# A gated mix of linear attention and a token-shift MLP on one core: the first four x tiles loaded as column slices and four query tiles accumulated side by side

## The chip, the cores and the metric

The kernel runs on one core of a Trainium2 chip. The metric is the device time of one execution in microseconds (us). Before the change the median of three runs is 259.72 us (259.62 to 259.99).

## The reference, cut to what matters

```python
x = A_x                                                 # 2048 x 640, bfloat16
g = sigmoid((x * gate_w).sum(-1, keepdims=True))
a = linear_attention(x, wqkv, wo)                       # phi(q), phi(k), 32 heads of 20
b = mixer_mlp(x, w1, w2, w3, w4)                        # layernorm, w1, shifts, w2, layernorm, w3, w4
return g * a + (1 - g) * b
# in linear_attention: qkv = x @ wqkv; phi(t) = where(t > 0, t + 1, exp(t)) + 1e-6
```

The change touches only the start of the attention branch: the loading of x and of the query and key parts of wqkv, the turning of x (TensorE needs x with its 640 features on the partitions), and the first query products x @ wq.

## The kernel before, in words

The 2048 tokens are 16 tiles of 128; the 640 features are 5 column blocks k of 128 (KD = 5). One query tile is five matmuls, one for each k, 128 x 512, added up in one PSUM bank: the stationary operand is the block xT[:, k, tile], the moving one wq[:, k, 0:512]. One key tile is five matmuls of 512 columns and five of 130 in a pair of banks. After its last matmul a query tile goes through `phi` (lines 788 to 796): an Exp on ScalarE, a TENSOR_SCALAR and a SCALAR_TENSOR_TENSOR on VectorE; only then is its bank free. The last 128 query columns are done for four tiles together (`q_turned`).

xT comes in two ways. For tiles 0 to 2 `t_x` (lines 777 to 786) transposes the five blocks on TensorE against an identity (`tr_group`, L615, five transposes in one bank) and VectorE copies them out of PSUM (`copy`, L669). For tiles 3 to 15 `x_turn` (line 689) has SP issue a DMA transpose as soon as the tile's load has landed. In the same bank as tile 2's transposes one small matmul turns the gate weights (line 782), and VectorE casts the result into wkg (line 786).

Every instruction is recorded by `_Sched`, which adds the semaphore waits that its reads, writes and PSUM banks need. Each engine then works off its own list strictly in the order recorded. `_Items.run` (line 336) decides that order from estimated costs: the stream "A" (lines 944 to 960) is warm-up matmuls without a use for the result (`warmup`, WARM = 3456 columns), t_x(0), 128 warm-up columns, then `q_three` (query tiles 0 to 2), `k_two` (key tiles 0 and 1), key tile 2, and from tile 3 on a query tile and a key tile in turn, with the turned query columns after every fourth key tile. Inside `q_three` and `k_two` the order is written out by hand as pairs (tile, k) and worked off by `stream` (line 906); there (t, None) means "turn tile t now".

Loads are issued in the order of lines 694 to 718, from the SP queue and the ACT queue. x tiles 0 to 3 are four loads of 160 KB each, in pieces of 1280 bytes; the five blocks wq[:, k, 0:512] are 128 KB each, in pieces of 1024 bytes; the five blocks of wk are 160 KB each.

`IT.add("QN", ...)` at line 1359 only makes the later scaling of the queries wait for the item that holds the first query tiles.

Of the kernel before, what the change touches and what calls it, by code (L numbers as in the profile page):

```python
# [11 lines left out]
D = 640  # L12
# [5 lines left out]
KD = D // 128  # L18
# [398 lines left out]
def _build(nc, A_x, A_wqkv, A_wo, B_w1, B_w2, B_w3, B_w4, gate_w, out, dbg=None, stop=None):  # L417
# [42 lines left out]
    ps = nc.alloc_psum_tensor("ps", [128, 8, 512], F32)  # L460
    sch.register(ps, "ps", 8 * PS_BANK, 0)

    def psb(b, n0, n1):
        return ps[:, b, :].bitcast(BF16)[:, n0:n1]
# [53 lines left out]
    def bank():  # L518
        best = None
        for k_ in range(nbanks[0]):  # L520
            b = (bank_rr[0] + k_) % nbanks[0]
            if b in bank_pend or b in bank_hold:
                continue
            lk = sch.locks.get(b)
            tfree = 0.0 if lk is None else sch.ev_time.get((lk[1].sem, lk[1].val), 1e18)
            if best is None or tfree < best[0]:
                best = (tfree, b)
        bank_rr[0] = best[1] + 1
        bank_pend.add(best[1])
        return best[1]  # L530
# [67 lines left out]
    def mm_group(out_ap, pairs, reads_extra=()):  # L598
        n = len(pairs)

        def fn(e, out_ap=out_ap, pairs=pairs, n=n):
            ins = None
            for i, (l, r) in enumerate(pairs):
                ins = e.matmul(out_ap, l, r, start=(i == 0), stop=(i == n - 1))  # L604
            return ins
        reads = [a for p in pairs for a in p] + list(reads_extra)
        return pe(fn, reads, [out_ap], cost=n * (max(nfree(pairs[0][1]), 24) * 0.4167 + 2.5))

    def tr_group(b, srcs):
        outs = [psb(b, 128 * i, 128 * (i + 1)) for i in range(len(srcs))]  # L610

        def fn(e, outs=outs, srcs=srcs):
            ins = None
            for o, s_ in zip(outs, srcs):
                ins = e.transpose(o, s_, ident[:])  # L615
            return ins
        return pe(fn, list(srcs) + [ident[:]], [psb(b, 0, 128 * len(srcs))], cost=len(srcs) * 56.0)
# [47 lines left out]
    def copy(engf, out_ap, in_ap):  # L665
        cost = None
        if engf is dve and in_ap.dtype == BF16 and out_ap.dtype == BF16:
            cost = 65.0 + nfree(out_ap) / 1.92
        return engf(lambda e: e.tensor_copy(out_ap, in_ap), [in_ap], [out_ap], cost=cost)  # L669
# [5 lines left out]
    x2 = A_x[0]  # L675

    def dma_in(out_ap, in_ap, key, **kw):
        return sch.dma("sp", out_ap, in_ap, key, **kw)

    def load_x(t):  # L680
        dma_in(x_tok[:, t, :], x2[128 * t:128 * (t + 1), :], "x%d" % t)

    def load_wq(k, queue):
        sch.dma(queue, wq[:, k, 0:512], A_wqkv[128 * k:128 * (k + 1), 0:512], "wq%d" % k)

    def load_wk(k, queue):
        sch.dma(queue, wkg[:, k, 0:D], A_wqkv[128 * k:128 * (k + 1), D:2 * D], "wk%d" % k)

    def x_turn(t):
        sch.dma("sp", xT[:, :, 128 * t:128 * (t + 1)], x_tok[:, t, :], "trx%d" % (t % 4), transpose=True)  # L690

    gwr = xn[:, 1, 0:128]
    dve(lambda e: e.memset(gwr, 0.0), [], [gwr])
    load_x(0)
    load_wq(0, "act")
    load_x(1)
    load_wq(1, "act")
    load_wq(2, "sp")
    load_wq(3, "act")
    load_x(2)  # L700
    load_wq(4, "act")
    load_wk(0, "sp")
    load_wk(1, "act")
    load_x(3)
    load_wk(3, "act")
    sch.dma("act", wq[:, :, 512:D], A_wqkv[:, 512:D].rearrange("(k p) f -> p k f", p=128), "wqt")
    load_wk(2, "sp")
    load_wk(4, "sp")
    load_x(4)
    x_turn(3)  # L710
    load_x(5)
    sch.dma("pool", xn[0:KD, 1, 0:128], gate_w.rearrange("(k p) -> k p", p=128), "gw")
    x_turn(4)
# [60 lines left out]
    WARM = 3456  # L774
    WARM2 = 128

    def t_x(t):
        for k0, k1 in ((0, 1), (1, KD)) if t < 2 else ((0, KD),):
            b = bank()
            tr_group(b, [x_tok[:, t, 128 * k:128 * (k + 1)] for k in range(k0, k1)])  # L780
            if t == 2:
                mm_group(ps[:, b, 448:448 + KD], [(gwr, ident[:, 0:KD])])
            for j0, j1 in {(1, 1): ((1, 3), (3, KD)), (2, 0): ((0, 2), (2, KD))}.get((t, k0), ((k0, k1),)):
                copy(dve, xT[:, j0:j1, 128 * t:128 * (t + 1)], psb(b, 128 * (j0 - k0), 128 * (j1 - k0)).rearrange("p (k c) -> p k c", k=j1 - j0))
            if t == 2:
                copy(dve, wkg[:, :, D + 1:D + 2], ps[:, b, 448:448 + KD].rearrange("p (k o) -> p k o", o=1))

    def phi(b, dst, after_exp=None, n=D):
        se = slot("E", 3)
# [86 lines left out]
    def warmup(cols, cyc):  # L876
        b = bank()
        one = nc.const_aps.tensor(1.0, [128, 512], BF16)
        steps = [512] * (cols // 512) + [128] * (cols % 512 // 128)

        def fn(e):
            ins = None
            for n in steps:
                ins = e.matmul(ps[:, b, 0:n], one[:, 0:128], one[:, 0:n], start=True, stop=True)  # L884
            return ins
        pe(fn, [], [ps[:, b, :]], cost=cols * cyc)
# [13 lines left out]
    def q_tile(t):  # L900
        tok = slice(128 * t, 128 * (t + 1))
        b = bank()
        mm_group(ps[:, b, :], [(xT[:, k, tok], wq[:, k, 0:512]) for k in range(KD)])
        phi(b, pq_tok[:, t + 1, 0:512], n=512)

    def stream(order, w, n2, done):
        bs = {}
        for t in sorted({t for t, k in order if k is not None}):
            bs[t] = pair() if n2 else bank()
            bank_hold.update((bs[t], bs[t] + 1) if n2 else (bs[t],))  # L910
        for t, k in order:
            if k is None:
                if t is None:
                    warmup(256, 0.42)
                else:
                    t_x(t)
                continue
            b = bs[t]
            l = xT[:, k, 128 * t:128 * (t + 1)]

            def fn(e, l=l, b=b, k=k):
                ins = e.matmul(ps[:, b, 0:512], l, w[:, k, 0:512], start=(k == 0), stop=(k == KD - 1))  # L922
                return ins if not n2 else e.matmul(ps[:, b + 1, 0:n2], l, w[:, k, 512:512 + n2], start=(k == 0), stop=(k == KD - 1))  # L923
            pe(fn, [w[:, k, 0:512 + n2], l], [ps[:, b, 0:512]] + ([ps[:, b + 1, 0:n2]] if n2 else []), cost=272.0 if n2 else 216.0)
            if k == KD - 1:
                bank_hold.difference_update((b, b + 1) if n2 else (b,))
                done(t, b)

    def q_three():
        order = [(0, 0), (1, None), (0, 1), (1, 0), (1, 1), (0, 2), (1, 2), (0, 3), (1, 3), (2, None), (0, 4), (1, 4),  # L930
                 (2, 0), (2, 1), (2, 2), (2, 3), (2, 4)]
        stream(order, wq, 0, lambda t, b: phi(b, pq_tok[:, t + 1, 0:512], n=512))

    def k_out(t, b):
# [6 lines left out]
    def addA(name, dur, fn, deps=()):  # L941
        IT.add("A", name, dur, fn, deps)
# [1 line left out]
    addA(("warm",), 0.0, lambda: warmup(WARM, 0.834))  # L944
    addA(("tx", 0), 0.28, lambda: t_x(0))
    addA(("warm", 1), 0.0, lambda: warmup(WARM2, 0.42))
    addA(("q", 2), 3.24, q_three)
    addA(("k", 1), 2.72, k_two)
    addA(("k", 2), 1.36, lambda: k_tile(2))
    for i in range(3, NT + 2):  # L950
        if i < NT:
            addA(("q", i), 1.08, lambda t=i: q_tile(t))
            addA(("k", i), 1.36, lambda t=i: k_tile(t))
            if i % 4 == 3:
                addA(("qx", i // 4), 1.08, lambda c=i // 4: q_turned(c))
                IT.add("QB", ("qb", i // 4), 0.0, lambda c=i // 4: q_back(c),
                       deps=[(("qx", i // 4), 2.5), (("t1", NT - 1), 0.0) if i == NT - 1 else (("k", i + 1), 0.0)])
        if i > 3:
            for t in range(3) if i == 4 else (i - 2,):
                addA(("g0", t), 0.27, lambda t=t: gt_tail(t), deps=[(("k", max(t, 1)), 2.0)])  # L960
# [355 lines left out]
    for t in range(NT):  # L1316
        c = t // 4
# [38 lines left out]
                    IT.add("W3", ("w3h", c2), 1.14, lambda c2=c2: w3_half(c2), [(("t2", u), 0.9) for u in range(4 * c2 + 4, 4 * c2 + 8)] + [(("a", 3), 0.0)])  # L1356
                IT.add("W3", ("w4h", 0), 0.76, lambda: w4_half(0), [(("w4load",), 0.0), (("a", 3), 0.0)])
    for t in range(NT):
        deps = [(("zb",), 1.0), (("q", max(t, 2)), 2.0), (("sg", 1), 0.0)]
        deps.append((("qb", t // 4), 3.0))  # L1360
        if t < 5:
            i = 4 * t + 3
            deps.append((("w1", i // KD, i % KD), 0.0))
        else:
            i = 3 * (t - 5)
            if t >= 12:
                deps.append((("w4", t - 12), 0.0))
            if t < 12:
                deps.append((("w3", i // KFF, i % KFF), 0.0))
        IT.add("QN", ("qs", t), 0.0, lambda t=t: qn_sum(t), deps)  # L1370
        IT.add("QN", ("qn", t), 0.0, lambda t=t: qn_scale(t), [(("qs", t), 0.0)])
        IT.add("QT", ("qt", t), 0.0, lambda t=t: qt_tile(t), deps=[(("qn", t), 3.2), (("w2", NT - 1), 0.5), (("t2", 11 if t < 6 else NT - 1), 0.0)] + ([(("mt",), 0.0)] if t == 3 else []))
# [70 lines left out]
```

## Time and profile before

| what | value |
|---|---|
| median of three runs | 259.72 us (259.62 to 259.99) |
| time of the profiled execution | 259.2 us |
| its span, first to last instruction | 257.9 us |
| TensorE (PE) busy | 255.1 us, 99% |
| VectorE (DVE), ScalarE (ACT), GpSimd (POOL) busy | 56%, 42%, 35% |
| moved by DMA | 26.50 MB, mean 103 GB/s over the span |
| DMA share and rate from 2.0 to 9.0 us | 1.00 to 1.12 in the four windows asked for, 302 to 349 GB/s |

The profile shows one execution. Times in it count from the start of the span. "PE" is the matmul, "PEld" the loading of a stationary operand, which overlaps PE; SPq and ACTq are the issuing of DMAs on these two queues. A matmul's duration runs to its modelled end and overlaps the next one's start, so what a matmul costs in a row of matmuls is the distance between two starts.

### The profile page before, as it was taken

How to read it: one execution, taken by the hardware profiler on the slowest of the kernel's cores; microseconds unless marked ns; L12 is line 12 of the kernel's file. 1: busy time of each engine (PE TensorE's matmuls, PEld its weight loads, DVE VectorE, ACT ScalarE, POOL GpSimd, SP SyncE). 2: the span in 40 equal slices, each digit the busy share in tenths (PEclk: the TensorE clock that was granted, in tenths of full speed). 3: DMA queues.
4: the chain of work that ended last, by engine and by line, in shares of the span. 5: the costliest groups of instructions: out<-in, count | busy, mean ns of one | idle time of the engine just before them, and what ended most of it. 6: DMA issues, size and time to landing. Idle time of an engine off the chain costs nothing.

```text
span 257.9 us, 3904 instructions
## 1 busy us (share of the span) xinstructions
PE 255.1 (99%) x1478; PEld 126.7 (49%) x1478; DVE 144.8 (56%) x289; ACT 108.9 (42%) x224; POOL 90.9 (35%) x144
## 2 busy tenths in 40 slices
PE   8999999999999999999999999999999999999996
PEld 4555555544454545555444445444444744444744
DVE  2697888899964995589999300399700033200033
ACT  1587676651366868666854331001540100253100
POOL 5020499976952162677908000123200021300000
PEclk9999999999999999999999999999999999999999
DMA  7856699956637699372628630114130022200012
GB/s 226 226 135 114 188 137 177 262 109 126 127 76 79 125 399 293 84 100 56 121 49 117 123 60 3 31 25 127 36 17 0 3 52 80 102 1 3 0 20 102
DMA packets 57650, 26.50 MB, mean 103 GB/s; under 512 B 48884, under 2 KB 56221, under 8 KB 57632
## 3 DMA queue, kind: packets, MB, share of 16 engines
q1 hardware_dynamic: 54800, 21.87, 40.2%
q0 software_dynamic: 1168, 3.28, 5.8%
q10 hardware_dynamic: 1664, 1.11, 1.4%
q8 instruction: 11, 0.18, 0.3%
q14 instruction: 7, 0.06, 0.1%
HBM read 12.04 MB, written 2.62 MB: 57 GB/s over the span
## 4 chain that ended last, share of the span: by engine, by line
PE 99%; DVE 0%; issue 0%
PE ps L604 53%; PE ps L1213 30%; PE ps L811 8%; PE ps L922 2%; PE ps L884 1%; PE ps L1240 1%; PE ps L1128 1%; PE ps L615 1%; PE ps L1009 0%; PE ps L1038 0%; PE ps L923 0%; DVE x_tok L643 0%
## 5 line engine op out<-in xcount | busy, mean ns | idle before, releaser
L604 PE MATMUL ps<-xnT,w 128*128 128x512 bf16 x360 | 81.3, 379 | 0.0
L643 DVE SCALAR_TENSOR_TENSOR x_tok<-ps,stg,abx 128x512 bf16<-128x512 f32 (+2 forms) x17 | 12.2, 718 | 81.4 <-PE ps L1213 81.3
L660 ACT ACTIVATE h2T<-ps 128x512 bf16<-128x512 f32 x52 | 30.6, 598 | 59.5 <-PE ps L604 59.5
L604 PEld LDWEIGHTS ps<-xnT,w 128*128 128x128 bf16 x360 | 34.5, 98 | 39.8 <-issue 0.5
L1213 PE MATMUL ps<-w,h2T 128*128 128x512 bf16 (+2 forms) x221 | 45.4, 366 | 0.0
L626 POOL TENSOR_SCALAR xn<-x_tok,st 128x640 bf16<-128x640 bf16 x32 | 36.0, 1130 | 25.4 <-DMA xnT<-xn 24.9
L626 POOL TENSOR_SCALAR abx<-x_tok,stg 128x640 f32<-128x640 bf16 x16 | 15.3, 965 | 70.7 <-DVE x_tok L643 70.7
L1213 PEld LDWEIGHTS ps<-w,h2T 128*128 128x128 bf16 x221 | 21.2, 98 | 23.5
L660 ACT ACTIVATE Er<-ps 128x512 bf16<-128x512 f32 (+1 forms) x36 | 23.0, 649 | 14.6 <-PE ps L604 10.3
L659 ACT ACTIVATE junk<-x_tok 128x640 bf16<-128x640 bf16 x32 | 23.6, 738 | 3.9 <-DVE x_tok L641 3.7
L660 ACT ACTIVATE hsT<-ps 128x512 bf16<-128x512 f32 (+1 forms) x32 | 19.0, 594 | 12.5 <-PE ps L604 12.0
L604 PE MATMUL ps<-w,hsT 128*128 128x512 bf16 (+1 forms) x160 | 23.7, 299 | 0.0
L604 PE MATMUL ps<-wkg,xT 128*128 128x130 bf16 (+1 forms) x140 | 21.4, 299 | 0.0
L641 DVE SCALAR_TENSOR_TENSOR x_tok<-ps,x_tok 128x640 bf16<-128x640 f32 x16 | 13.1, 821 | 11.2 <-PE ps L604 10.5
L604 PEld LDWEIGHTS ps<-w,hsT 128*128 128x128 bf16 x160 | 13.3, 98 | 12.3
L1213 PE MATMUL ps<-M_sb,pqnT 128*128 128x512 bf16 (+2 forms) x85 | 18.6, 367 | 0.0
L811 PE MATMUL ps<-pk_tok,x_tok 128*128 128x512 bf16 x80 | 17.8, 379 | 0.0
L604 PEld LDWEIGHTS ps<-wkg,xT 128*128 128x128 bf16 x140 | 11.9, 97 | 11.4
L1157 DVE TENSOR_TENSOR pq_tok<-pq_tok,dnr 128x300 bf16<-128x300 bf16 (+1 forms) x48 | 16.9, 405 | 0.5
L634 DVE TENSOR_TENSOR qprod<-qprod,pk_tok 128x640 f32<-128x640 f32 x13 | 16.3, 1252 | 0.4
L626 DVE TENSOR_SCALAR Er<-Er 128x512 bf16<-128x512 bf16 (+1 forms) x36 | 12.3, 341 | 6.9 <-ACT Er L660 6.2
L604 PE MATMUL ps<-wq,xT 128*128 128x512 bf16 x65 | 16.2, 379 | 0.0
(87 smaller groups left out, 243.8 us busy)
## 6 DMA issues: line engine op xcount, KB each, us to landing
w<-in_B_w_dram SPq DMA_DIRECT2D x1, 2160.0 KB, 8.1
w<-in_B_w_dram SPq DMA_DIRECT2D x1, 2080.0 KB, 15.2
out_dram<-x_tok SPq DMA_DIRECT2D x3, 640.0 KB, 3.2
w<-in_B_w_dram POOLq DMA_DIRECT2D x8, 160.0 KB, 6.4
x_tok<-in_A_x_dram SPq DMA_DIRECT2D x6, 160.0 KB, 3.7
x_tok<-in_A_x_dram SPq DMA_DIRECT2D x1, 960.0 KB, 5.3
wv<-in_A_wqkv_dram POOLq DMA_DIRECT2D x1, 800.0 KB, 5.7
x_tok<-in_A_x_dram SPq DMA_DIRECT2D x1, 640.0 KB, 4.6
```

The lines of the kernel that those rows point to most:

```text
L604: ins = e.matmul(out_ap, l, r, start=(i == 0), stop=(i == n - 1))
L615: ins = e.transpose(o, s_, ident[:])
L626: return engf(lambda e: e.tensor_scalar(out_ap, in_ap, s1, s2, op0, op1), rd, [out_ap], cost=cost)
L634: return engf(lambda e: e.tensor_tensor(out_ap, a, b_, op), [a, b_], [out_ap], cost=cost)
L641: return dve(lambda e: e.scalar_tensor_tensor(out_ap, in0, scalar, in1, op0, op1, accum_out=accum), rd, [out_ap, accum], cost=cost + 70.0)
L643: return dve(lambda e: e.scalar_tensor_tensor(out_ap, in0, scalar, in1, op0, op1), rd, [out_ap], cost=cost)
L659: return act(lambda e: e.activation(out_ap, in_ap, func, bias=bias, scale=scale, accum_out=accum), rd, wr, cost=cost)
L660: return act(lambda e: e.activation(out_ap, in_ap, func, bias=bias, scale=scale), rd, wr, cost=cost)
L811: ins = e.matmul(o, l, r, start=(t0 + q_ == 0), stop=(t0 + q_ == NT - 1))
L922: ins = e.matmul(ps[:, b, 0:512], l, w[:, k, 0:512], start=(k == 0), stop=(k == KD - 1))
L1157: dve(lambda e, o=o, i0=i0, i1=i1: e.tensor_tensor(o, i0, i1, ALU.mult), [i0, dnr[:, 1, sd, :]], [o], cost=cost)
L1213: ins = e.matmul(o, l, r, start=first and i == 0, stop=last and i == len(prs) - 1, skip_group_check=True)
```

## The change

x tiles 0 to 3 are loaded by three DMAs, each with a slice of the columns of all four tiles: block 0 (128 KB in pieces of 256 bytes), blocks 1 and 2 (256 KB in pieces of 512 bytes), blocks 3 and 4 (the same). They stand on SP; wq's blocks 0 to 2 stand beside them on ACT, and all wq loads are on ACT now. wk's blocks 0, 2 and 4 follow on SP. `x_turn(3)` is gone.

`t_x(k)` now turns block k of four tiles: four transposes in one bank, and a copy of 512 columns (for block 0 a copy of 128 and one of 384). The gate weights' matmul and cast are in t_x(3). `q_three` becomes `q_four`, with the four banks of query tiles 0 to 3 open together and (None, k) for "turn block k now"; the single query tile 3 that stood between key tiles 2 and 3 is gone.

```diff
-    load_x(0)
-    load_wq(0, "act")
-    load_x(1)
-    load_wq(1, "act")
-    load_wq(2, "sp")
+    for i, (k0, k1) in enumerate(((0, 1), (1, 3), (3, KD))):
+        dma_in(x_tok[:, 0:4, 128 * k0:128 * k1], x2[0:512, 128 * k0:128 * k1].rearrange("(n p) d -> p n d", p=128), "xs%d" % i)
+        load_wq(i, "act")
     load_wq(3, "act")
-    load_x(2)
+    load_wk(0, "sp")
     load_wq(4, "act")
-    load_wk(0, "sp")
+    load_wk(2, "sp")
     load_wk(1, "act")
-    load_x(3)
+    load_wk(4, "sp")
     load_wk(3, "act")
     sch.dma("act", wq[:, :, 512:D], ...)
-    load_wk(2, "sp")
-    load_wk(4, "sp")
     load_x(4)
-    x_turn(3)
     load_x(5)
...
+    def t_x(k):
+        b = bank()
+        tr_group(b, [x_tok[:, t, 128 * k:128 * (k + 1)] for t in range(4)])
+        if k == 3:
+            mm_group(ps[:, b, 448:448 + KD], [(gwr, ident[:, 0:KD])])
+        for j0, j1 in ((0, 1), (1, 4)) if k == 0 else ((0, 4),):
+            copy(dve, xT[:, k, 128 * j0:128 * j1], psb(b, 128 * j0, 128 * j1))
+        if k == 3:
+            copy(dve, wkg[:, :, D + 1:D + 2], ps[:, b, 448:448 + KD].rearrange("p (k o) -> p k o", o=1))
...
-        order = [(0, 0), (1, None), (0, 1), (1, 0), (1, 1), (0, 2), (1, 2), (0, 3), (1, 3), (2, None), (0, 4), (1, 4),
-                 (2, 0), (2, 1), (2, 2), (2, 3), (2, 4)]
+        order = [(0, 0), (1, 0), (None, 1), (2, 0), (3, 0), (0, 1), (1, 1), (None, 2), (2, 1), (3, 1), (0, 2), (1, 2), (None, 3), (2, 2),
+                 (None, 4), (3, 2)] + [(t, k) for t in range(4) for k in (3, 4)]
...
-    addA(("q", 2), 3.24, q_three)
+    addA(("q", 3), 4.32, q_four)
...
-            addA(("q", i), 1.08, lambda t=i: q_tile(t))
+            if i > 3:
+                addA(("q", i), 1.08, lambda t=i: q_tile(t))
...
-        deps = [(("zb",), 1.0), (("q", max(t, 2)), 2.0), (("sg", 1), 0.0)]
+        deps = [(("zb",), 1.0), (("q", max(t, 3)), 2.0), (("sg", 1), 0.0)]
```

After the key tiles 2 and 3 the instructions of the changed program stand in the same order as before on TensorE, to the end.

More of the change, by code (lines that the diff above doesn't have):

```diff
@@ L775, in _build @@
     WARM2 = 128
[L777 to L786, printed above, removed]
+    def t_x(k):
[7 more added lines that the diff above has]
+            copy(dve, wkg[:, :, D + 1:D + 2], ps[:, b, 448:448 + KD].rearrange("p (k o) -> p k o", o=1))
     def phi(b, dst, after_exp=None, n=D):
@@ L907, in stream @@
         bs = {}
-        for t in sorted({t for t, k in order if k is not None}):
+        for t in sorted({t for t, k in order if t is not None}):
             bs[t] = pair() if n2 else bank()
@@ L911, in stream @@
         for t, k in order:
[L912 to L916, printed above, removed]
+            if t is None:
+                t_x(k)
                 continue
@@ L927, in stream, with q_four @@
                 done(t, b)
-    def q_three():
-        order = [(0, 0), (1, None), (0, 1), (1, 0), (1, 1), (0, 2), (1, 2), (0, 3), (1, 3), (2, None), (0, 4), (1, 4),
-                 (2, 0), (2, 1), (2, 2), (2, 3), (2, 4)]
+    def q_four():
+        order = [(0, 0), (1, 0), (None, 1), (2, 0), (3, 0), (0, 1), (1, 1), (None, 2), (2, 1), (3, 1), (0, 2), (1, 2), (None, 3), (2, 2),
+                 (None, 4), (3, 2)] + [(t, k) for t in range(4) for k in (3, 4)]
         stream(order, wq, 0, lambda t, b: phi(b, pq_tok[:, t + 1, 0:512], n=512))
```

## The prediction, made before the changed kernel ran

> **What bounds the kernel now.** I read the page's busy times and its chain, then the chain in order of time, then the timeline of the first 9 us, then the DMA issues of that stretch.
>
> ```profile
> PE 255.1 (99%) x1478; PEld 126.7 (49%) x1478; DVE 144.8 (56%) x289; ACT 108.9 (42%) x224; POOL 90.9 (35%) x144
> ...
> PE 99%; DVE 0%; issue 0%
> ```
>
> TensorE is the bound from end to end. A busy PE need not be a full one, so I looked at the distances between matmul starts: after 8.96 us, where the first key matmul starts, none shows a wait. What counts is when that first key matmul starts, and how much PE work is left then. The chain in order of time gives the prices:
>
> ```profile
> 3.87 0.53 PE ps L615 x5
> ...
> 5.50 1.67 PE ps L922 x7
> 7.17 0.28 PE ps L615 x5
> ...
> 20.00 2.44 PE ps L604 x15
> ...
> 25.43 3.52 PE ps L604 x20
> ```
>
> Five transposes take 0.53 us early and 0.28 later: 0.107 and 0.056 each. The clock doubles in between. Of 20.00 and 25.43 the difference is one group of five 128x512 matmuls, 1.08 us: 0.216 each; cold it is 0.43 (the warm-up's weight loads stand at 2.07, 2.49, 2.92). Matmul starts keep the cold distance until 5.3 and have the warm one from 5.71.
>
> The second thing to see is what a transpose costs before its result can be used:
>
> ```profile
> 4.09 0.31 PE L615 MATMUL ps<-ident,x_tok 128*128 128x128 bf16 x1
> ...
> 4.38 0.59 PE L922 MATMUL ps<-wq,xT 128*128 128x512 bf16 x1
> ```
>
> ```profile
> 4.01 0.22 DVE L669 COPY xT<-ps 128x128 bf16<-128x128 bf16 x1 [3.03 <-PE ps L615]
> 4.44 0.43 DVE L669 COPY xT<-ps 128x512 bf16<-128x512 bf16 x1 [0.20 <-PE ps L615]
> ...
> 7.52 0.55 DVE L669 COPY xT<-ps 128x256 bf16<-128x256 bf16 x2 [1.49 <-PE ps L604]
> 8.00 0.17 DVE L669 CAST wkg<-ps 128x5 bf16<-128x5 f32 x1
> ```
>
> ```profile
> 7.29 0.17 PE L604 MATMUL ps<-ident,xn 128*128 128x5 bf16 x1
> ...
> 7.87 0.76 PEld L922 LDWEIGHTS ps<-wq,xT 128*128 128x128 bf16 x5 [0.45 <-DVE xT L669]
> ...
> 8.96 0.38 PE L922 MATMUL ps<-wkg,xT 128*128 128x512 bf16 x1
> ```
>
> A copy starts 0.35 us after the last transpose's start when cold (4.09 to 4.44), 0.23 when warm (7.29 to 7.52). 512 columns take 0.43. The weight load follows 0.05 to 0.08 after the copy's end (the first copy of 7.52 lasts 0.29, to 7.81; the load starts at 7.87). So warm it is 0.23 + 0.43 + 0.07 = **0.73 us from the last of four transposes to the first matmul with them**, 0.90 from the first. Before the change almost all of this lies under other matmuls: the one wait left is 0.12 us (the matmul before 7.87 started at 7.53 and occupies 0.216).
>
> **The change, part by part.** Times from the span's start; t1 is the start of the second slice's transposes, r that of block 3's.
>
> *Start.* The warm-up stays and holds PE until 3.68, where tile 0's transposes now start; x tile 0 landed 2.8 us after its issue at 0.79. If slice 0 is no later, four cold transposes start at 3.68 to 4.00, the first copy runs 4.35 to 4.57, and matmul (0,0) starts 0.15 later (as 4.24 to 4.38), at 4.72. Two cold matmuls of 0.43 end at 5.58. The 128 warm-up columns fill 0.11 of the gap; some 0.4 us of PE idles.
>
> *Slice 1.* Its transposes need blocks 1 and 2 of all four tiles. All loads share a DMA side that is full (share 1.00 to 1.12 from 2 to 9 us):
>
> ```profile
> x_tok<-in_A_x_dram SPq DMA_DIRECT2D x1, 160.0 KB, 2.8
> ```
>
> ```profile
> x_tok<-in_A_x_dram SPq DMA_DIRECT2D x1, 160.0 KB, 4.3
> wq<-in_A_wqkv_dram SPq DMA_DIRECT2D x1, 128.0 KB, 4.0
> ```
>
> These are tile 0, and the third and fourth SP loads: wq's block 2 issued at 1.71, tile 2 at 2.18, so landing at 5.7 and 6.5. SP had then brought 448 and 608 KB; tile 1, at 4.3, made 320. Slice 1 completes 384 KB on SP. Bounds: 4.3, and 6.5 if short pieces slow it. I take 5.75, the wq row that stands nearest, so t1 = 5.80. Slice 2 completes 640 KB: between tile 2 (6.5) and tile 3 (3.13 + 5.6 = 8.7); I take 7.4. It is needed at r.
>
> *The side-by-side order, warm.* Block 1: four transposes (0.22), (2,0) and (3,0) (0.43): PE is through at t1 + 0.65, but (0,1) can start at t1 + 0.90. **Bubble 0.25.** (0,1), (1,1) to t1 + 1.33. Block 2 the same: bubble 0.25, (0,2) at t1 + 2.23, (1,2) done at t1 + 2.66 = r = 8.46. Block 3: transposes to r + 0.22, gate matmul 0.03, (2,2), block 4's transposes, (3,2) to r + 0.90: there (0,3) is just ready. VectorE, however, copies block 3 from r + 0.40 to 0.83, casts the gate to 1.00, and only then copies block 4, to 1.43; (0,4) starts at r + 1.50, where (0,3) ended at 1.12. **Bubble 0.38.** Then seven matmuls from (0,4) on, 1.51: the first key matmul starts at r + 3.01 = **11.47**. Check: from 5.80, 16 transposes 0.89, 18 matmuls 3.88, gate 0.03, bubbles 0.88: 5.68.
>
> *What is saved.* The lone query tile 3: five matmuls, 1.08 us. The old program, with that tile ahead, would have its keys at 8.96 + 1.08 = 10.04. **Net: 11.47 - 10.04 = +1.43 us**, all of it on the path, since no later wait of PE's can absorb it.
>
> *Moved, priced at nothing.* The DMA transpose of tile 3 (1.30 us of SP, from 8.75) goes; behind it tiles 5 and 4 come no later, and tile 4's turned x, needed at about 18 us, was ready near 13.5 (landing 10.8, transpose 2.7): nothing becomes late. The wk blocks landed at 7.8 to 10.3 and are needed from 11.5 to 13.4; cover over 1 us. ACT has one more issue of 0.46 us before its table load (done 5.42); its first Exp is due after 10. Four query tiles now reach phi together: Exp 0.59 each, VectorE 0.29 + 0.69 each. Key tile 1 takes tile 0's bank at its first matmul, 2.33 us after (0,4) starts; the old (0,4), at 7.32, had its phi done at 9.38, 2.06 after. Cover 0.2 us; if it is gone, PE waits for the excess. The next banks have over 1 us.
>
> *A rule against the change.* The Trainium skill, "TensorE: Matmul & The Clock Gate", Part 1, says that the clock opens after about 3.4 us of sustained activity, in a window that runs free. This trace agrees in so far as starts were 0.43 us apart until 5.3 us, with PE busy without a gap since 0.83. The change puts about half a microsecond of idling into that stretch; by the rule read strictly the opening could slip by a window, and my sum would be +2.6 rather than +1.4. No row shows how large a gap it tolerates. A second rule, "DMA: Bandwidth & Descriptors", Specifications, wants transfers of 512 bytes or more for full rate: slice 0, in pieces of 256, falls below; the page gives no factor.
>
> What a trace row says of short pieces is only a bound: 640 KB of x in 512 pieces landed 4.6 us after issue, 160 KB in 128 pieces as little as 2.5. Slice 0 has 512 pieces and 128 KB, so it lands between 3.3 and 5.4. I take no later than tile 0 did, nearest in size and place; 5.4 would add up to 1.7 us at the start.
>
> **Rivals.**
> 1. *Late slices.* By the upper bounds (slice 0 at 5.4, or slice 1 at 6.5 and slice 2 past 9) the keys start 0.7 to 1.7 later: +2.1 to +3.1. For it: the DMA side is full and pieces shrink. Against: the same bytes.
> 2. *The clock opens late.* If everything up to r runs cold, eight transposes cost 0.05 more each and eight matmuls 0.21 more each, 2.1, less the 0.5 of bubbles and some of the waits that they fill: r slips by about 1.2, sum +2.6. For it: the idling named. Against: PE is still busy four fifths of the time.
> 3. *Not slower: the bubbles close.* The place is the path transpose, copy, matmul. If it takes 0.48 us instead of 0.73 (as two matmuls cover) and block 4's copy does not queue behind the cast, the 0.88 goes and slice 1 lands by 5.55: +0.3, which is within 0.2%. Against: the copy alone is 0.43. For a gain, the five added transposes (0.28) would have to vanish as well, and no wait of before is left that could pay for it.
>
> **How the numbers follow.** The profiled execution took 259.2 us, 0.5 below the median of the three runs; from it the sum is 260.6, from the median 261.15. I name 261.2, to be set against 259.72. 0.2%, about what a measurement of this kernel can tell from no change, is 0.52 us. Chances: forecast, +0.8 to +2.0, 0.64; late slices 0.17; late clock 0.09; bubbles closed 0.06, nearly all within 0.2%; a gain over 0.2% by something not seen 0.02; worse than all 0.02. The range, +0.7 to +3.1, is 260.4 to 262.8: it takes in rivals 1 and 2 and leaves out 0.1. Faster 0.02, same 0.07, slower 0.91.
>
> **What would show it.** Right: weight loads of wq waiting for the copies of L669 three times, 0.2 to 0.4 us each; the first key matmul near 11.5; no PE wait after it; the span longer by the same amount. Wrong: the first key matmul at 10.5 or earlier; matmul starts 0.43 apart beyond 6 us (rival 2); transposes waiting for the slices' DMA for more than 0.3 us (rival 1); or a PE wait for pq_tok's bank in key tile 1.

## The result, and the profile after

| kernel | median, us | lowest to highest | ratio to the kernel before, 95% interval |
|---|---|---|---|
| before, beside it | 259.67 (12 runs) | 259.11 to 263.07 | |
| changed | 260.98 (12 runs) | 260.44 to 262.33 | 1.0049 [1.0029, 1.0068] |

The changed kernel is **slower by 1.3 us, or 0.5%**. 261.2 was predicted, a loss of 1.4 to 1.5.

Two numbers of a trace carry all that follows: where the first key matmul starts, and how long it is from there to the start of the last matmul of all.

| profiled execution, us | span | first transpose | first key matmul | from there to the last matmul |
|---|---|---|---|---|
| before | 257.9 | 3.68 | 8.96 | 246.74 |
| changed | 259.2 | 3.87 | 11.30 | 245.66 |

The last column differs by 1.08, the five matmuls of the lone query tile 3, which the changed kernel has ahead of its keys. In sum nothing else changed behind the first key matmul. The whole loss is therefore made ahead of it: 11.30 - 8.96 - 1.08 = 1.26 us, and the spans differ by 1.3.

The timeline of TensorE's matmuls in the changed kernel, from 3.8 us on (columns: start, duration, engine, line, operation, operands, count, and in brackets the wait ahead of it):

```profile
3.87 0.61 PE L615 MATMUL ps<-ident,x_tok 128*128 128x128 bf16 x4
4.27 0.31 PE L878 MATMUL ps<-const-bfloat16-1.0 128*128 128x128 bf16 x1
4.88 0.59 PE L913 MATMUL ps<-wq,xT 128*128 128x512 bf16 x2 [0.30 <-DVE xT L669]
5.31 0.38 PE L615 MATMUL ps<-ident,x_tok 128*128 128x128 bf16 x4
5.53 0.59 PE L913 MATMUL ps<-wq,xT 128*128 128x512 bf16 x2
6.31 0.59 PE L913 MATMUL ps<-wq,xT 128*128 128x512 bf16 x2 [0.18 <-DVE xT L669]
6.74 0.39 PE L615 MATMUL ps<-ident,x_tok 128*128 128x128 bf16 x4
6.96 0.59 PE L913 MATMUL ps<-wq,xT 128*128 128x512 bf16 x2
7.73 0.59 PE L913 MATMUL ps<-wq,xT 128*128 128x512 bf16 x2 [0.18 <-DVE xT L669]
8.32 0.40 PE L615 MATMUL ps<-ident,x_tok 128*128 128x128 bf16 x4
...
11.30 0.38 PE L913 MATMUL ps<-wkg,xT 128*128 128x512 bf16 x1
```

The pattern repeats: four transposes, two matmuls of the block before, then a wait for a copy. Read the wait from starts, not from the bracket: the two matmuls at 5.53 take 0.216 each and would be through at 5.97, and the next one starts at 6.31. That is 0.34 us without work; the bracket shows 0.18, since modelled ends reach past the next start. The same 0.34 stands before 7.73. Behind block 3 and block 4 there are 0.13 and 0.21 more (starts at 9.37 and 9.79, inside a group that is not shown). The four come to **1.02 us**.

What VectorE did meanwhile, in the same kernel:

```profile
5.74 0.42 DVE L669 COPY xT<-ps 128x512 bf16<-128x512 bf16 x1 [0.73 <-PE ps L615]
7.16 0.42 DVE L669 COPY xT<-ps 128x512 bf16<-128x512 bf16 x1 [1.00 <-PE ps L615]
8.79 0.42 DVE L669 COPY xT<-ps 128x512 bf16<-128x512 bf16 x1 [1.21 <-PE ps L604]
9.13 0.17 DVE L669 CAST wkg<-ps 128x5 bf16<-128x5 f32 x1
9.22 0.42 DVE L669 COPY xT<-ps 128x512 bf16<-128x512 bf16 x1
```

And the weight loads for the products with the copied blocks:

```profile
6.28 0.13 PEld L913 LDWEIGHTS ps<-wq,xT 128*128 128x128 bf16 x2 [0.64 <-issue]
...
9.34 0.10 PEld L913 LDWEIGHTS ps<-wq,xT 128*128 128x128 bf16 x1 [0.27 <-issue]
9.76 1.21 PEld L913 LDWEIGHTS ps<-wq,xT 128*128 128x128 bf16 x7 [0.33 <-issue]
```

Every copy waits for its transposes, and TensorE waits for the copy: a serial chain. (The brackets of these weight loads say "issue", but each stands 0.12 behind the end of a copy, and the matmuls at 6.31 and 7.73 name the copy.) From the last transpose's start at 5.48 the copy starts 0.26 later, lasts 0.42, the weight load follows 0.12 behind it and the matmul 0.03 behind that: 0.83 us. The last transpose itself (0.06) and two matmuls (0.43) cover 0.49 of it; 0.34 is left open.

### The profile page after: what moved, and what is told of

The parts are those of the page before. It is cut to its first block, busy times and chain, and to the rows that moved or that the text cites. A ratio compares the mean times of both kernels' runs of the same rounds, so it can differ in the third digit from the quotient of the medians.

```text
span 259.2 us, 3885 instructions
## 1 busy us (share of the span) xinstructions
PE 254.2 (98%) x1457; PEld 126.6 (49%) x1483; DVE 143.9 (56%) x288; ACT 108.7 (42%) x224; POOL 90.2 (35%) x144
## 3 DMA queue, kind: packets, MB, share of 16 engines
q10 hardware_dynamic: 1808, 1.25, 1.7%
## 4 chain that ended last, share of the span: by engine, by line
PE 96%; ACT 2%; DVE 1%; issue 1%
PE ps L604 50%; PE ps L1205 30%; PE ps L805 8%; PE ps L913 2%; PE ps L878 1%; PE ps L1232 1%; ACT hsT L660 1%; PE ps L1120 1%; PE ps L615 1%; DVE xT L669 0%; PE ps L1001 0%; PE ps L1030 0%; ACT junk L659 0%; DVE pk_tok L643 0%; ACT Er L660 0%
## 5 line engine op out<-in xcount | busy, mean ns | idle before, releaser
L604 PE MATMUL ps<-xnT,w 128*128 128x512 bf16 x349 | 79.9, 379 | 0.5 <-issue 0.2
L1205 PE MATMUL ps<-w,h2T 128*128 128x512 bf16 (+2 forms) x216 | 44.7, 366 | 0.3
L626 POOL TENSOR_SCALAR xn<-x_tok,st 128x640 bf16<-128x640 bf16 x32 | 35.2, 1106 | 26.8 <-DMA xnT<-xn 26.3
L604 PE MATMUL ps<-w,hsT 128*128 128x128 bf16 (+1 forms) x159 | 23.5, 298 | 0.2
L604 PE MATMUL ps<-wq,xT 128*128 128x512 bf16 x57 | 14.8, 379 | 0.2
```

Of the source, the lines that this page charges most:

```text
L626: return engf(lambda e: e.tensor_scalar(out_ap, in_ap, s1, s2, op0, op1), rd, [out_ap], cost=cost)
L1205: ins = e.matmul(o, l, r, start=first and i == 0, stop=last and i == len(prs) - 1, skip_group_check=True)
```

## The experiments

All kernels compute the whole reference. Five of them, called late, have a longer warm-up and start their first transpose 8 to 9 us later, so that the loads have landed and the clock has opened before the first transpose; what is left is the order of the work alone. In them "first transpose to first key matmul" is the measure: the start of the first transpose moves with the opening of the clock from run to run (11.92 to 12.85 in these five), and this distance leaves that out.

### The changed order without loads and clock: the changed kernel and the kernel before, both started late

```diff
-    addA(("warm",), 0.0, lambda: warmup(WARM, 0.834))
+    addA(("warm",), 0.0, lambda: warmup(WARM + 18944, 0.834 * WARM / (WARM + 18944)))
```

The changed kernel with this edit:

> The changed kernel with 37 more warm-up matmuls ahead (18944 columns, planned at the old cost so that the order stays): TensorE begins its real work only near 12 us, when all of x tiles 0 to 3, wq and wk have landed and the clock is open. To be read against e4, which does the same to the kernel before. If the order on PE is the cause (bubbles and transposes), e3 stays 1.2 us behind e4: from the end of the warm-up to the first key matmul 6.9 us here. If late slices or the cold clock are the cause, e3 is at most 0.3 to 0.5 us behind e4.

The kernel before with this edit:

> The kernel before with the same 37 warm-up matmuls. From the end of the warm-up to the first key matmul 4.6 us, all warm. PE order as the cause: 1.2 us less than e3 after the tile 3 that e3 has done already (1.08 us) is counted. Slices or clock as the cause: 0.3 to 0.5 us less.

The changed kernel, late, on TensorE:

```profile
12.60 0.39 PE L615 MATMUL ps<-ident,x_tok 128*128 128x128 bf16 x4
...
14.82 0.59 PE L913 MATMUL ps<-wq,xT 128*128 128x512 bf16 x2 [0.18 <-DVE xT L669]
...
16.24 0.59 PE L913 MATMUL ps<-wq,xT 128*128 128x512 bf16 x2 [0.18 <-DVE xT L669]
...
19.63 0.38 PE L913 MATMUL ps<-wkg,xT 128*128 128x512 bf16 x1
```

The kernel before, late:

```profile
12.47 0.44 PE L615 MATMUL ps<-ident,x_tok 128*128 128x128 bf16 x5
...
17.18 0.38 PE L922 MATMUL ps<-wkg,xT 128*128 128x512 bf16 x1
```

From the first transpose to the keys it is 7.04 and 4.71; less the 1.08 that query tile 3 takes, the order costs **1.25 us** with every load landed and the clock open. That is as much as the loss of the kernels as they are (1.26). That the two agree so closely is partly luck: loads and clock are not without a price in the kernels as they are, but it was about the same in these two executions. The changed kernel's first transpose starts 0.19 later, and it takes 7.44 - 7.04 = 0.40 longer to its keys than when late, 0.59 together; the kernel before takes 5.28 - 4.71 = 0.57 longer. The 1.25 consists of five more transposes (5 x 0.0555 = 0.28); the same waits of 0.34, 0.34, 0.13 and 0.21 against 0.04, 0.07 and 0.13 in the late kernel before, 0.78 more; and 0.22 in the opening, where the weight load of the first product starts 0.60 after the first transpose in the kernel before and 0.76 in the changed one, though it has one transpose less ahead of it (0.055). Sum 1.28. By medians the pair differs by 268.84 - 267.82 = 1.02, with four runs each, spread over 0.6 to 0.7 us; the changing start of the first transpose is in these.

### The waits closed by another order

```diff
-        order = [(0, 0), (1, 0), (None, 1), (2, 0), (3, 0), (0, 1), (1, 1), (None, 2), (2, 1), (3, 1), (0, 2), (1, 2), (None, 3), (2, 2),
-                 (None, 4), (3, 2)] + ...
+        order = [(0, 0), (1, 0), (None, 1), (None, 2), (2, 0), (3, 0), (0, 1), (1, 1), (2, 1), (3, 1), (0, 2), (1, 2), (None, 3), (None, 4),
+                 (2, 2), (3, 2)] + ...
...
-        if k == 3:
+        if k == 4:      # the cast of the gate weights, behind block 4's copy
```

> The changed kernel with the transposes of block 2 right behind those of block 1, block 4's right behind block 3's, and the gate's cast after the copy of block 4, so that four matmuls stand between each copy and its use. If the three bubbles were all (1.02 us of waits on copies in the changed kernel's profile), the first key matmul comes 0.8 us earlier, at 10.5, span 258.4. If slice 2's landing (8.28 us) holds PE as well, PE only reaches it earlier and waits: first key matmul near 11.05, span 259.0, PE idle before block 3's transposes some 0.7 us. If neither matters and only the clock or the late start did: 11.3 and 259.2 as before.

260.23 us, ratio 1.0026 [1.0015, 1.0038]: 0.75 less than the changed kernel. In its profiled execution the keys came at 11.06 although the clock opened 1.4 us later (the first matmul at the full rate starts at 6.29 against 4.88). The waits between blocks were 0.06, 0.13 and 0.12. 11.06 is also what was expected if slice 2 held TensorE, but that is a coincidence: slice 2 landed at 8.07 and its first transpose starts at 8.19, right behind the matmul before it. The same order started late:

> The order of e2 (bubbles covered) with the long warm-up of e3: neither the slices' landing nor the opening of the clock is in the way. e3 took 7.04 us from its first transpose to its first key matmul, with four waits on copies of 0.34, 0.34, 0.13 and 0.21 us. If these waits are the cause, 6.3 us here (0.06 + 0.12 + 0.12 of waits left). If they are not, 7.0.

```profile
13.67 0.61 PE L615 MATMUL ps<-ident,x_tok 128*128 128x128 bf16 x8
14.12 2.00 PE L916 MATMUL ps<-wq,xT 128*128 128x512 bf16 x8
...
18.82 0.38 PE L916 MATMUL ps<-wkg,xT 128*128 128x512 bf16 x1
```

Eight transposes in a row, then eight matmuls with one wait of 0.12 among them instead of two of 0.34: 6.38 us to the keys, 0.66 less than the changed order. So the waits behind the copies make half of the loss, and another order takes most of them away. What is left, 6.38 - 4.71 - 1.08 = 0.59, is the five transposes, the opening and 0.1 of waits.

### The gate's cast alone

The changed kernel, late, with nothing but the cast behind block 4's copy:

```diff
-        if k == 3:
+        if k == 4:
             copy(dve, wkg[:, :, D + 1:D + 2], ...)
```

> The changed kernel with the long warm-up of e3 and one edit: the gate's cast stands on VectorE after the copy of block 4 instead of before it. My prediction priced the cast's place at 0.17 us of the third bubble. By the copies' starts in the changed kernel's profile (a copy starts 0.34 after the one before it, with the cast between 0.43) it is only 0.09: first transpose to first key matmul 6.95 us against e3's 7.04. By the prediction's price 6.87.

```profile
16.44 0.85 DVE L669 COPY xT<-ps 128x512 bf16<-128x512 bf16 x2 [1.03 <-PE ps L604]
17.21 0.17 DVE L669 CAST wkg<-ps 128x5 bf16<-128x5 f32 x1
```

A miss: 7.04 us to the keys, as without the edit. The two copies now start 0.43 apart (16.44 and 16.87), and with the cast between them they started 0.43 apart all the same (17.13 and 17.56 in the late changed kernel). Block 4's copy starts 0.26 after the last of its own transposes, as block 1's and block 2's copies do after theirs. The cast lies in VectorE's time of waiting and costs nothing.

### Tile 3 on TensorE in the old order

Two kernels ask what the five transposes cost by themselves. First the kernel before, with tile 3 turned on TensorE just ahead of key tile 2:

```diff
-    x_turn(3)
...
+    addA(("tx", 3), 0.28, lambda: t_x(3))
     addA(("k", 2), ...
```

> The kernel before with one part of the change alone: x tile 3 is turned on TensorE (five transposes ahead of key tile 2, copied under it) instead of by SP's DMA transpose. My account of the +1.3 us has 0.28 us for five more transposes (5 x 0.056): first key matmul as before near 9.0 us, span +0.3 us (258.2), ratio 1.001. Rival, that the turning on TensorE brings a wait of its own (a copy in the way of phi on VectorE, a bank): +0.6 us or more. If transposes cost nothing because PE has slack that the profile hides: 0.

261.73 us, ratio 1.0082 [1.0056, 1.0109]: no better than the changed kernel, and not by the transposes. TensorE in this kernel:

```profile
12.71 0.66 PE L604 MATMUL ps<-wkg,xT 128*128 128x512 bf16 x6
14.96 1.25 PE L604 MATMUL ps<-wq,xT 128*128 128x512 bf16 x5 [1.59 <-DVE xT L669]
```

and VectorE ahead of that wait:

```profile
13.68 0.83 DVE L643 SCALAR_TENSOR_TENSOR pk_tok<-ps,Er 128x640 bf16<-128x640 f32 x1
14.43 0.48 DVE L669 COPY xT<-ps 128x640 bf16<-128x640 bf16 x1
```

The transposes stood at 11.56, but their copy was recorded behind phi of key tiles 0 and 1, and VectorE works in that order: it came at 14.43, and query tile 3 waited 1.6 us. My placing was at fault. It shows the same chain at a larger price. The mended form, late, turns tile 3 at the end of `q_three` and is set against the late kernel before:

```diff
-    x_turn(3)
...
-                 (2, 0), (2, 1), (2, 2), (2, 3), (2, 4)]
+                 (2, 0), (2, 1), (2, 2), (2, 3), (2, 4), (3, None)]
```

> The kernel before with the long warm-up of e4, and tile 3 turned on TensorE at the end of the three query tiles (in e1 it stood after the two key tiles, and its copy waited on VectorE behind their phi). Five transposes at 0.056: from first transpose to first key matmul 4.99 us against e4's 4.71, and the copy done before query tile 3 needs it, so no wait of PE's after it. If turning on PE costs more than its PE time wherever it stands, a wait before query tile 3 as in e1 (1.6 us there).

The keys come 4.99 us after the first transpose against 4.71: 0.28, the transposes' own time. Behind the first key matmul 0.31 more was lost, at key tile 1's first weight load, which waits for the phi of a query tile:

```profile
18.96 0.10 PEld L921 LDWEIGHTS ps<-wkg,xT 128*128 128x128 bf16 x1 [0.47 <-DVE pq_tok L643]
```

I put this down to the transposes' bank, which shifts the turn of the banks by one; no run separates it. (One run.) Turning tile 3 on TensorE costs 0.28 at the least where TensorE has no gap to put it in.

### The idle gap in the opening, filled

```diff
-    WARM2 = 128
+    WARM2 = 512
```

> The changed kernel with 512 instead of 128 warm-up columns between slice 0's transposes and the first query matmul: the half microsecond in which PE idled there is filled, nothing else moves. If that idling delays the clock (rival 2 of the prediction), matmul starts have the warm distance earlier than in the changed kernel, and the median falls by some tenths of a us, ratio 1.003. If not, the time stays where it was: ratio 1.005.

260.75 us, ratio 1.0044 [1.0016, 1.0071], which is the changed kernel's within either interval. In the profiled execution the clock opened early (the full rate from 3.97 on), but the added columns stand at 4.21, behind that, so this opening is not their doing; that the filling is worth nothing rests on the times. Nor did the early clock help: slice 2 landed at 8.80, and the weight loads for its transposes show what came instead:

```profile
8.84 0.23 PEld L615 LDWEIGHTS ps<-ident,x_tok 128*128 128x128 bf16 x4 [1.09 <-DMA x_tok<-in_A_x_dram]
```

TensorE itself stood for 0.76 us there, and the keys came at 11.82, later than in the changed kernel's profile. Here the early clock only brought TensorE to the wait for slice 2 earlier.

### The loads

The closed order, with slice 2 cut in two: block 3 on SP and block 4 on ACT, ahead of wq's block 3.

```diff
-    for i, (k0, k1) in enumerate(((0, 1), (1, 3), (3, KD))):
+    for i, (k0, k1) in enumerate(((0, 1), (1, 3), (3, 4))):
...
+    sch.dma("act", x_tok[:, 0:4, 512:640], x2[0:512, 512:640]..., "xs3")
     load_wq(3, "act")
```

> e2 with slice 2 halved by columns: block 3 (128 KB, pieces of 256 bytes) stays on SP behind slice 1, block 4 goes on ACT ahead of wq's blocks 3 and 4. In e2, in the changed kernel and in e8 slice 2 landed at 8.07, 8.28 and 8.80 us, and PE waited for it where it came early to block 3 (0.76 us in e8). If slice 2's place in the queue is what makes it late, block 3 lands by 7.5 and block 4 by 8.0, no PE wait ahead of block 3, but wq's block 3 may now be late by some tenths; time as e2 or up to 0.3 us less, ratio 1.002. If the whole DMA side is short of rate, the wait only moves to block 4 or wq and the time is that of e2, 1.0026, or worse. It stays slower than the kernel before in either case: five more transposes are 0.28 us.

260.46 us, ratio 1.0023 [1.0009, 1.0036], the closed order's own. Block 3 landed at 6.96, more than 1 us earlier, and block 4 at 7.99, but wq's blocks 3 and 4, now behind it, landed at 8.83 and 9.44 (7.26 and 8.01 in the closed order). The list of waits of this kernel, from 3 to 12 us (total, times, longest):

```profile
PEld ps L917 <- DMA wq<-in_A_wqkv_dram: 1.0, 2, 0.5
PE ps L917 <- DMA wq<-in_A_wqkv_dram: 0.2, 1, 0.2
```

The wait moved from x to wq: what is ahead on a full DMA side is paid for by what is behind. And the changed kernel with all that is left of x in one load of 512 KB, in pieces of 1024 bytes:

```diff
-    for i, (k0, k1) in enumerate(((0, 1), (1, 3), (3, KD))):
+    for i, (k0, k1) in enumerate(((0, 1), (1, KD))):
...
+    load_wq(2, "act")
```

> The changed kernel with blocks 1 to 4 as one load of 512 KB in pieces of 1024 bytes instead of two in pieces of 512. A look at the DMA side alone: the same bytes stand in the same place on SP. If pieces of 512 bytes are what makes slice 2 late, the one load lands near 7.5 us, 0.6 earlier than slice 2 (8.1 to 8.8 in three profiles). If it is the bytes of both queues, it lands at 8.1 to 8.8 as well. PE must wait for all of it before block 1, so the keys start later than in the changed kernel, at 12 us or after, whatever the cause.

261.38 us (one run); the keys at 12.21, since block 1's transposes now wait for the whole load. But it landed at 6.33 us, where the same 512 KB in two loads were complete only at 8.07, 8.28 and 8.80 (closed order, changed kernel, filled gap). The stretch from 4 to 6 us, each engine's busy time, then granted clock, DMA share and GB/s, of the changed kernel:

```profile
4.00:6.00 2.00, 1.70 (x13) 0.90 (x11) 0.75 (x3) 1.14 (x1) 0.71 (x5) 1.00 0.96 255
```

of the kernel with the single load:

```profile
4.00:6.00 2.00, 1.20 (x7) 0.56 (x7) 0.49 (x2) 1.07 (x1) 0.72 (x5) 1.00 1.07 343
```

and of the kernel before:

```profile
4.00:6.00 2.00, 2.00 (x14) 1.17 (x13) 1.33 (x5) 1.28 (x1) 0.72 (x5) 1.00 1.00 328
```

The DMA engines are as good as fully busy in all three, and bring 255 against 343 and 328 GB/s. Over all profiles the stretch has 236 to 289 GB/s in the six kernels whose slices 1 and 2 both come in pieces of 512 bytes, and 301 to 347 in the five without pieces of 512 bytes: on average a fifth less.

The rate alone does not explain 2 us, however. In this stretch SP's queue moved 0.52 of 0.69 MB with the single load and 0.29 of 0.51 MB in the changed kernel, so it also had a larger share, at the cost of ACT's queue. The single load also has its second half issued 0.54 us earlier (1.31 against 1.85). Which of piece size and the single issue gave SP the larger share, no run separates. And a landing is that of the last of 16 DMA engines: in the changed kernel thirteen of them had their part of slice 2 in by 7.27, the last at 8.28.

None of these kernels beats the kernel before. Between its blocks that one has 0.24 us of waits when the loads are out of the way, less than the 0.28 of the added transposes.

## Why the prediction was right, step by step

*Where the loss is made.* Right: ahead of the first key matmul, which came at 11.30 (predicted 11.47), and nothing behind it. Net 1.26 against 1.43 predicted. Steps that erred up and down make up the 0.17, and that they cancel so far is luck:

| step | predicted | measured | effect on the keys |
|---|---|---|---|
| first product (0,0) | 4.72 | 4.88, as slice 0 landed at 3.82 | +0.16 |
| first two products | 0.86, cold | 0.43, the clock was open | -0.43 |
| slice 1 awaited | until 5.80 | not; it landed at 5.08 | -0.22 |
| from there to block 3's transposes | 2.66 | 3.01 | +0.35 |
| from there to the keys | 3.01 | 2.98 | -0.03 |

*The bubbles.* The mechanism was right, and the late pair shows it by itself. The size was short: the chain from the last transpose takes 0.83 us, not 0.73. Of the terms, the start of the copy was 0.26 instead of 0.23, the weight load followed 0.12 behind the copy instead of 0.07, and the matmul 0.03 behind the load, where I had nothing. The 0.23 was a misreading: the row at 7.29 is the gate's small matmul, which this copy also waited for; the last transpose of that bank starts at 7.23. The first two bubbles are 0.34 and not 0.25.

*The third bubble.* The time was right ((0,4) at r + 1.47, predicted 1.50), **the cause was wrong**. I had block 4's copy queue behind the gate's cast. My price for VectorE was too high: the next instruction starts 0.34 after a copy and 0.09 after the cast (8.79, 9.13, 9.22), where I had 0.43 and 0.17. So what holds block 4's copy is its own transposes, which stand behind (2,2), and moving the cast changed nothing. The bubble also falls into two parts, 0.13 before (0,3) and 0.21 before (0,4), as (0,3) was not "just ready".

*The five transposes.* 0.28, confirmed by the old order with tile 3 turned in time (4.99 - 4.71). Saved for query tile 3: 1.08, confirmed to 0.01.

*The opening.* That the first copy waits for four transposes, where the kernel before has tile 0's first transpose in a group of its own, was in the sum: the first product was put 1.04 us after the first transpose, came 1.01 after it, and in the kernel before 0.71. Warm, in the late pair, the difference is worth 0.22. The idling ahead of the first product, which I put at some 0.4, is 0.5 by my own times (4.72 less 4.21) and was 0.51.

*The landings.* Both were wrong, by 0.7 and 0.9 in opposite directions (5.08 for 5.75; 8.28 for 7.4). I had counted bytes per queue. The errors did not decide: slice 1 was early, and slice 2 was reached so late, because of the bubbles, that TensorE stood only 0.16 us for it. Slice 0, put at no later than tile 0 had been, held TensorE for another 0.20 us ahead of the first transpose. Rival 1's mechanism was there, under cover. The sign that I named for it, transposes waiting over 0.3 us for a slice, stands in the weight load's row at 8.32 (0.49 us for the DMA), but TensorE's own wait there is the 0.16. Where the cover goes, as in the kernel with the filled gap, it shows (0.76).

*Costs set at nothing.* The profile after has no wait behind 9.79 up to the end of key tile 1, neither for pq_tok's bank nor for wk. The 0.2 us of cover for phi held here; in the old order with tile 3 turned early, where the banks' turn is moved by one, it was gone.

*Rival 2, the late clock.* It did not happen. In this execution the last start at half rate is at 4.27 and the first at the full rate is (0,0) itself, at 4.88, with 0.20 us of idling ahead of the first transpose and 0.51 ahead of (0,0); in the kernel before, without such gaps, it is 5.71. In 12 profiles the first start at the full rate lies between 3.97 and 6.29; the five late kernels, which start alike and keep TensorE busy without a gap up to their first transpose, alone spread from 4.08 to 5.89. So the spread is one of executions, and the idle gap leaves no mark that stands out from it. The Trainium skill, "TensorE: Matmul & The Clock Gate", Part 1, calls the window free-running, with a spread of 500 ns to either side; a spread is what these runs show, of 0.9 us to either side among the five with the same gapless start, and the strict reading that a gap restarts the count is not supported: in the kernel with the split load a gap of 0.36 us ended at 4.03, and the full rate came at 4.30.

*Rival 3.* The path took 0.83 us where it would have had to take 0.48. With another order around it, the loss fell to 0.26%, not to nothing: as the rival said, the five transposes stay.

*Short pieces.* I took the smallest slice, with its 256-byte pieces, to be the one at risk. It landed in 3.0 us, near the lower end. The late one was slice 2, in 512-byte pieces; slice 1, in the same pieces, was early. The Trainium skill, "DMA: Bandwidth & Descriptors", Specifications, asks for 512 bytes at least for full rate; here 512 did not reach it (236 to 289 GB/s from 4 to 6 us, against 301 to 347 without pieces of 512 bytes, at shares of 0.92 to 1.05 and 1.00 to 1.07). My remark that the page gives no factor holds for that section, not for the whole page.

What stays open: how much the early and late openings weigh in the medians. Between single executions the opening differs by up to 2.3 us, and the net of the profiled pair (1.26) agrees with that of the medians (1.31) although the changed one has its first start at the full rate 0.8 us earlier. That part of this advantage was spent waiting, as with the filled gap, is likely, but not separated. Nor did a run change the opening alone; its 0.22 is read from starts.

## What to carry to other kernels

An operand of 512 columns that is turned on TensorE at the full rate and copied out comes back 0.83 us after the last transpose; put at least that much other TensorE work between the two: two matmuls of 512 columns left 0.34 us open each time, two blocks turned at once and eight matmuls behind them 0.12 in all. In a head of the kernel that has no gap, work that is moved from a DMA to TensorE is paid for in full (0.28 of 0.28 us, one run). Recording a copy late on a busy engine can cost more than the work that it serves (1.6 us for a copy of 0.48).

## What the runs showed of the hardware that was not expected

- On a full DMA side the rate goes with the piece size: from 2 to 8 us packets of 256, 512, 1024 and 1280 bytes took 18, 27, 46 and 55 ns of one DMA engine (medians, the same in every profile), so 512 bytes run at 19 bytes per ns and 1280 at 23. The rates by stretch differ somewhat more (255 against 328).
- One load of 512 KB in pieces of 1024 bytes was complete 1.7 to 2.5 us before the same bytes in two loads of 512-byte pieces (one run against three; its queue also had a larger share of the DMA engines, 77% of their time against 54%).
- The doubling of the matmul rate comes 3.1 to 5.5 us after the warm-up's beginning (0.83 us), and over 1.8 us of that range with the same work ahead of it. The granted clock stands at 1.00 from 4 to 6 us of the kernel before, where starts are 0.43 apart until 5.3: only the distances between starts show the doubling.
